# Another order for the unit schedule of a fused attention and feed-forward kernel: other engines for casts and transposes, v loads ahead of q and k, more zero matmuls

## The chip, the cores and the metric

The kernel runs on one core of a Trainium2 chip. Times are device microseconds (us) of one execution, input in HBM to output in HBM; the figure that is compared is the median of the runs. In the profile the engines are PE (TensorE's matmuls), PEld (its weight loads), DVE (VectorE), ACT (ScalarE), POOL (GpSimd) and SP (SyncE, which only issues transfers). Every engine works through its own queue in order, and waits on semaphores for the others.

## The reference

Attention with 4 batches, 8 heads, 768 positions and a head size of 64, followed by a feed-forward layer on 3072 tokens of width 512:

```python
scores = scale * np.matmul(q, k.transpose(0, 1, 3, 2))
keep = is_global | is_local          # k among the first 8, or 0 <= q - k < 96
scores = np.where(keep, scores - slope[h] * dist, -1e9)
a = softmax(scores)
x = (a @ v)  -> [3072, 512]
h = np.maximum(np.maximum(x @ w1, x @ w2), x @ w3)     # 512 -> 768, three times
out = h @ w_out                                        # 768 -> 512
```

A query sees at most its own block of 128 positions, the one before, and the first 8 positions of its batch. All inputs and the output are float32; the kernel computes in bfloat16 with float32 sums.

## The kernel before

The tokens are cut into 24 tiles T of 128 (six to a batch, t = T mod 6). The program is a list of short units, `SCHEDULE`, and the loop of lines 475 and 476 emits them one after the other. Units of one engine run in the order of the list; nothing reorders them. Each unit writes tiles from pools with few buffers (lines 102 to 117), and an instruction that needs a buffer waits until its last reader is done. The last number of most units names an engine: 0 ScalarE, 1 VectorE, 2 GpSimd; 3 and 4 have meanings of their own.

Loads, all issued by SyncE in list order: `l n.s` (`load_part`, line 158) loads a part of q or k for a group of tiles; groups 0, 1 and 2 are the tile pairs 0-1, 2-3 and 4-5, with part 0 the q and part 1 the k; groups 3 and 4 are tiles 6-9 and 10-11. `L T` loads q and k of one later tile, `v T` its v, `w g.j` and `o i` the feed-forward weights. The parts l0.0 and l0.1 are issued ahead of the list (lines 439 and 440).

Casts to bfloat16: `c` (line 183) and `C T.0` (line 198; 3 splits it between VectorE and GpSimd) for q and k, `C T.1` (line 189) for v, `W` and `Q` for weights. Transposes of q and k into `qkT`: `x n.s` (lines 239 and 243) and `X T` (lines 261 to 266) on PE with a copy out of PSUM, where `x` with 3 uses one VectorE copy and with 4 one half copy each by ScalarE and VectorE; `X T.4` is instead one DMA transpose issued by SyncE (line 250), with no PE work and no copy.

Attention of tile T: `S T.g` is the scores of four heads, each score bank (psS, tags sp0 and sp1, one buffer each) holding two key blocks, and the exponential on ScalarE (line 288). With a 1 at its end the mask is added by two PE matmuls of a bias (line 275); with a 0 the product is masked by `M T.g` on VectorE (line 307). `K h` and `B h` make the mask and the bias of head h out of distances. `G` and `V` copy the first eight keys and values of the batch into the previous tile's place (lines 214, 216, 221). `A T.b` multiplies by v into score bank b (lines 322 and 325) and divides on VectorE (lines 331 and 332) into `xb`. `T T` transposes the result into `xT`: on PE with a copy (lines 349 and 350) or, with 4, by a DMA transpose (line 340).

Feed-forward, on chunks of 4, 2, 2, 4, 4, 4 and 4 tiles: `F c.f.j` is one of three products for one of six 128-wide parts of the hidden layer, four matmuls (line 361) into one of three `psH` buffers; j = 0 is copied out by ScalarE (line 366), j = 1 and 2 are folded in by VectorE maxima (lines 368 and 370). `O c.i` is a tile's output (six matmuls, line 376), its copy (line 382) and its store by SyncE (line 383). `E` is the last chunk's output. `D i.n` issues n matmuls of zeros (line 436).

Of the kernel before, what the change touches and what calls it, by code (L numbers as in the profile page):

```python
# [22 lines left out]


SCHEDULE = """
    K0 K1 K2 K3 K4 K5 l1.0 l1.1 D0.3 c0.0.2 B0.1 B1.1 B2.1 B3.0 K6 B4.1 B5.1 c0.1.1 c1.0.2 x0.0.4 B6.1
    B7.1 x0.1.4 S0.0.1 v0 l2.0 l2.1 K7 S0.1.1 G0.0 S1.0.1 S1.1.0 x1.0.3 c1.1.2 M0.0 M0.1 M1.0 v1 x1.1.4
    C0.1.2 v2 A0.1 G1.2 S2.0.1 M1.1 c2.0.2 x2.0.1 C1.1.1 S2.1.0 G2.2 S3.0.1 M2.0 M2.1 C2.1.1 T0.1 S3.1.1
    M3.0 M3.1 c2.1.2 v3 A1.0 C3.1.0 w0.0 V1.2 x2.1.2 w1.0 A2.1 V2.2 A3.0 T1.0 T2.1 T3.1 W1.0.1 W0.0.0
    G3.2 S4.0.0 S4.1.0 F0.0.0 F0.1.0 M4.0 F0.2.0 F0.3.0 G4.1 S5.0.0 M4.1 S5.1.0 w0.1 W0.1.1 w0.2 W0.2.2  # L30
    V3.2 F0.0.1 F0.1.1 F0.0.2 F0.1.2 v4 C4.1.0 A4.0 V4.2 w1.1 W1.1.2 W2.0.0 F0.4.0 F0.5.0 M5.0 M5.1 w1.2
    W1.2.2 v5 W2.1.0 T4.0 F0.2.1 F0.3.1 l3.0 l3.2 F0.4.1 l3.1 c3.0.2 c3.2.2 F0.5.1 o2 C5.1.0 A5.1 l3.3
    F0.2.2 Q2.2 F0.3.2 W2.2.0 o0 T5.0 F0.4.2 o1 F0.5.2 x3.0.0 F1.0.0 F1.1.0 c3.1.1 F1.2.0 x3.2.0 Q0.2
    F1.0.1 F1.1.1 F1.2.1 l4.0 l4.1 c3.3.0 F1.0.2 F1.1.2 F1.2.2 x3.1.2 x3.3.1 F1.3.0 F1.4.0 Q1.2 F1.3.1
    S6.0.0 S6.1.0 v6 v7 v8 G6.0 F1.3.2 F1.5.0 v9 c4.0.1 F1.4.1 S7.0.0 S7.1.0 G7.2 v10 M6.0 M6.1 M7.0
    M7.1 O0.0.0 F1.4.2 c4.1.1 C6.1.2 C7.1.2 L12 F1.5.1 S8.0.0 S8.1.0 x4.0.0 O0.1.0 A6.0 x4.1.2 A7.1 V7.2
    F1.5.2 v11 T6.0 O0.2.0 T7.1 G8.2 C8.1.2 S9.0.0 S9.1.0 G9.1 v12 v13 O0.3.0 F2.0.0 F2.1.0 S10.0.0 M8.0
    M8.1 M9.0 M9.1 S10.1.0 C9.1.2 L13 L14 F2.0.1 F2.1.1 F2.0.2 A8.0 C12.0.1 F2.1.2 G10.2 O1.0.0 V8.2
    A9.1 X12.1 M10.0 M10.1 C10.1.0 C11.1.0 F2.2.0 S11.0.0 S11.1.0 M11.0 M11.1 L15 F2.3.0 F2.4.0 O1.1.0
    V9.2 A10.1 F2.2.1 V10.2 T8.0 F2.3.1 F2.5.0 T9.0 A11.1 F2.4.1 T10.0 F2.2.2 F2.3.2 T11.1 F2.4.2  # L40
    S12.0.0 S12.1.0 F2.5.1 C13.0.2 C14.0.2 C15.0.1 X13.4 F3.0.0 F3.1.0 F3.0.1 G12.1 C12.1.0 F3.2.0
    F3.1.1 F3.2.1 S13.0.0 S13.1.0 F2.5.2 v14 C13.1.0 C14.1.2 M12.0 M12.1 F3.0.2 F3.1.2 X14.4 F3.2.2
    X15.4 G13.2 M13.0 M13.1 S14.0.0 S14.1.0 F3.3.0 F3.4.0 F3.5.0 M14.0 M14.1 G14.1 A12.0 A13.1 F3.3.1
    F3.4.1 F3.5.1 S15.0.0 M15.0 S15.1.0 G15.0 v15 V13.2 L16 L17 v16 T12.4 v17 M15.1 O2.0.0 C15.1.0 A14.0
    V14.2 F3.3.2 F3.4.2 T13.4 F3.5.2 C16.1.0 C16.0.2 X16.3 T14.4 C17.0.2 A15.1 X17.4 O2.1.0 S16.0.0
    S16.1.0 G16.1 L18 V15.2 L19 T15.1 M16.0 O3.0.0 M16.1 F4.0.0 F4.1.0 F4.0.1 F4.1.1 C18.0.2 L20 C19.0.2
    A16.1 F4.2.0 F4.3.0 S17.0.0 S17.1.0 F4.2.1 F4.0.2 F4.3.1 v18 M17.0 v19 M17.1 X18.3 X19.4 C20.0.0
    V16.2 F4.1.2 C17.1.2 O3.1.1 A17.1 F4.2.2 F4.3.2 S18.0.0 M18.0 S18.1.0 M18.1 F4.4.0 T16.4 T17.4
    F4.4.1 C18.1.2 C19.1.1 F4.4.2 X20.4 G18.1 S19.0.0 S19.1.0 F4.5.0 L21 M19.0 M19.1 v20 F4.5.1 A18.0
    T18.4 F4.5.2 A19.1 T19.4 V19.1 C21.0.1 X21.4 G19.1 L22 C22.0.2 L23 X22.4 O3.2.1 O3.3.0 O4.0.1  # L50
    S20.0.0 S20.1.0 M20.0 G20.0 O4.1.0 F5.0.0 F5.1.0 F5.2.0 S21.0.0 S21.1.0 G21.2 F5.0.1 F5.1.1 M20.1
    M21.0 F5.3.0 F5.0.2 F5.1.2 F5.2.1 F5.2.2 v21 C20.1.1 C21.1.2 F5.4.0 S22.0.0 M21.1 S22.1.0 C23.0.0
    F5.3.1 M22.0 M22.1 F5.5.0 F5.3.2 A20.0 V20.2 G22.2 v22 F5.4.1 X23.4 v23 F5.5.1 T20.4 A21.1 V21.1
    T21.4 F5.4.2 F5.5.2 S23.0.0 S23.1.0 M23.0 O4.2.0 M23.1 C22.1.2 A22.0 C23.1.0 O4.3.0 V22.2 T22.4
    A23.1 T23.4 O5.0.1 O5.1.0 O5.2.1 O5.3.0 F6.0.0 F6.1.0 F6.0.1 F6.0.2 F6.2.0 F6.3.0 F6.4.0 F6.1.1
    F6.2.1 F6.1.2 F6.3.1 F6.4.1 F6.2.2 F6.3.2 F6.5.0 F6.4.2 F6.5.1 F6.5.2 E
"""


# [1 line left out]
def kernel(  # L61
# [272 lines left out]

    def u_XT(T, how):
        c, i = where[T]
        if i == 0:
            xT[c] = xT_pool.tile([128, NP, len(chunks[c]) * 128], BF16, name="xT", tag="xT")
        if how == 4:
            nc.sync.dma_start_transpose(out=xT[c][:, :, i * 128:(i + 1) * 128],  # L340
                                        in_=xb[T].rearrange("p h d -> p (h d)"))
            return
        if early(T):
            tp = psH.tile([128, NP, 128], BF16, name="xtp", tag="h")
        else:
            tp = psT.tile([128, NP, 128], BF16, name="xtp", tag="tp")
        x = xb[T].rearrange("p h d -> p (h d)")
        for jp in range(NP):
            nc.tensor.transpose(tp[:, jp], x[:, jp * 128:(jp + 1) * 128], identb)  # L349
# [4 lines left out]

    def u_F1(c, f, j):
        W = len(chunks[c]) * 128
        if f == 0 and j == 0:
            ht[c] = ht_pool.tile([128, NF, W], BF16, name="ht", tag="ht")
        ps = psH.tile([128, W], FP32, name="h", tag="h")
        for dm in range(4):  # L360
            nc.tensor.matmul(ps, w123[f // 2][:, dm, j, (f % 2) * 128:(f % 2) * 128 + 128],  # L361
                             xT[c][:, dm], start=(dm == 0), stop=(dm == 3))
# [147 lines left out]
```

## Time and profile before

| What | Value |
|---|---|
| median of 3 runs | 180.04 us (179.69 to 180.06) |
| span of the profiled execution | 178.3 us, first to last instruction |
| the profiled execution's own total | not given by the page; the runs' median is 1.74 us over the span |
| PE busy | 166.9 us, 94% |
| VectorE, ScalarE, GpSimd busy | 118.9, 103.1, 37.5 us |
| mean granted TensorE clock | 0.997 |
| moved by DMA | 35.52 MB, mean 199 GB/s |
| DMA transposes issued by SyncE | 11 into xT, 9 into qkT |

Busy time is the union of an engine's instructions, and matmuls overlap one another, so a mean duration of a matmul is longer than what it takes of PE. The start of a row is counted from the span's beginning. An "idle before" names what ended an engine's wait. The chain of waits is followed back from the last instruction, each step to what released it.

### The profile page before, as it was taken

The numbers are of one execution on the slowest core, as the hardware profiler recorded it, in microseconds if no ns is written. First come the engines' busy times: TensorE is split into PE (matmuls) and PEld (weight loads), VectorE is DVE, ScalarE is ACT, GpSimd is POOL, SyncE is SP. The second block draws the span as 40 slices with busy tenths as digits, with TensorE's granted clock in tenths as the row PEclk, the third lists the DMA queues.
The fourth block names the chain that finished last, engine by engine and source line by source line (L and its number), as shares of the span: only waits on it lengthen the run. The fifth ranks groups of instructions, "written<-read, shape, count | busy, mean of one in ns | idle before, by whom it ended". The sixth has DMA issues, their size and how long they took to land.

```text
span 178.3 us, 3960 instructions
## 1 busy us (share of the span) xinstructions
PE 166.9 (94%) x1529; PEld 95.8 (54%) x1551; DVE 118.9 (67%) x237; ACT 103.1 (58%) x160; POOL 37.5 (21%) x65
## 2 busy tenths in 40 slices
PE   3599799999999999999999999999999999999992
PEld 0455644558867677845555555545444555444442
DVE  4519875986787689748979447979358896136620
ACT  4867898646689858555744837351772643341122
POOL 4355203543343112310007024100020401000000
PEclk9999999999999999999999999999999999999998
DMA  5999999999998999989544999769889674610006
GB/s 140 292 271 242 357 320 384 320 361 358 251 193 213 229 254 236 174 171 233 94 90 118 159 247 235 157 132 186 173 153 294 136 143 146 224 42 4 0 11 226
DMA packets 83587, 35.52 MB, mean 199 GB/s; under 512 B 66160, under 2 KB 78320, under 8 KB 83568
## 3 DMA queue, kind: packets, MB, share of 16 engines
q1 hardware_dynamic: 83424, 35.20, 82.8%
q8 instruction: 12, 0.20, 0.5%
q10 hardware_dynamic: 144, 0.07, 0.1%
q14 instruction: 7, 0.06, 0.1%
HBM read 25.17 MB, written 6.29 MB: 176 GB/s over the span
## 4 chain that ended last, share of the span: by engine, by line
PE 85%; DMA 8%; SPq 2%; issue 1%; POOL 1%; DVE 1%; ACT 1%; ACTq 0%
PE h L361 53%; PE po L376 17%; PE sp L283 6%; DMA rawv<-in_v_dram 4%; DMA rawp<-in_q_dram 4%; PE op L322 3%; PE op L325 2%; SPq L174 2%; PE tpp L239 2%; PE xtp L349 1%; SPq L158 1%; POOL qkp L183 1%; PE tp L261 1%; DVE xb L332 0%; ACT va L189 0%
## 5 line engine op out<-in xcount | busy, mean ns | idle before, releaser
L361 PE MATMUL h<-xT,w 128*128 128x512 bf16 (+1 forms) x491 | 99.2, 348 | 0.7 <-issue 0.2
L361 PEld LDWEIGHTS <-w 128*128 128x128 bf16 x504 | 46.9, 98 | 40.5 <-DVE w L427 0.3
L288 ACT ACTIVATE P<-sp 128x1024 bf16<-128x1024 f32 (+1 forms) x48 | 43.4, 955 | 20.6 <-PE sp L283 20.4
L368 DVE TENSOR_TENSOR h<-h,h 128x512 bf16<-128x512 bf16 (+1 forms) x42 | 25.3, 610 | 25.7 <-PE h L361 16.5
L366 ACT CAST h<-h 128x512 bf16<-128x512 f32 (+1 forms) x42 | 21.6, 533 | 21.5 <-PE h L361 21.3
L376 PE MATMUL po<-wo,ht 128*128 128x512 bf16 (+2 forms) x147 | 33.1, 362 | 0.5
L370 DVE TENSOR_TENSOR ht<-h,h 128x512 bf16<-128x512 bf16 (+1 forms) x42 | 25.1, 607 | 3.7 <-PE h L361 3.0
L307 DVE TENSOR_TENSOR P<-P,wmask 128x1024 bf16<-128x1024 bf16 x36 | 24.8, 718 | 3.6 <-ACT P L288 3.5
L376 PEld LDWEIGHTS <-ht 128*128 128x128 bf16 x156 | 14.0, 98 | 13.9
L382 ACT COPY ost<-po 128x512 f32<-128x512 f32 (+2 forms) x20 | 11.2, 564 | 17.8 <-PE po L376 17.7
L332 DVE TENSOR_TENSOR xb<-op,rz 128x512 bf16<-128x512 f32 x24 | 16.6, 692 | 0.8
L283 PEld LDWEIGHTS <-qkT 64*128 64x128 bf16 x352 | 10.2, 96 | 10.0 <-issue 8.0
L283 PE MATMUL sp<-qkT 64*128 64x128 bf16 x352 | 15.2, 223 | 0.4 <-DVE xb L332 0.4
L322 PEld LDWEIGHTS <-P 128*128 128x128 bf16 x192 | 12.5, 97 | 2.5 <-ACT P L288 0.2
L221 POOL COPY va<-vaf 8x260 int32<-8x260 int32 x14 | 6.3, 452 | 34.5 <-PE op L325 34.5
L198 POOL CAST qkb<-raw 128x1024 bf16<-128x1024 f32 x7 | 7.2, 1037 | 27.7 <-DMA raw<-in_q_dram 18.9
L322 PE MATMUL op<-va,P 128*128 128x65 bf16 x160 | 12.3, 193 | 0.7 <-ACT va L189 0.6
L239 PE MATMUL tpp<-identb,qkp 128*128 128x128 bf16 x96 | 8.5, 246 | 4.0 <-POOL qkp L183 3.4
L325 PEld LDWEIGHTS <-P 128*128 128x128 bf16 x160 | 10.4, 97 | 2.2 <-issue 0.7
L239 PEld LDWEIGHTS <-qkp 128*128 128x128 bf16 x96 | 7.0, 111 | 5.8 <-POOL qkp L183 4.3
L325 PE MATMUL op<-va,P 128*128 128x65 bf16 x128 | 9.9, 193 | 0.0
L243 ACT COPY qkT<-tpp 128x1024 bf16<-128x1024 bf16 (+1 forms) x9 | 7.9, 874 | 3.4 <-PE tpp L239 3.4
(66 smaller groups left out, 107.5 us busy)
## 6 DMA issues: line engine op xcount, KB each, us to landing
rawv<-in_v_dram SPq DMA_DIRECT2D x24, 256.0 KB, 4.8
out_dram<-ost SPq DMA_DIRECT2D x23, 256.0 KB, 2.3
rawp<-in_q_dram SPq DMA_DIRECT2D x6, 512.0 KB, 7.2
rawp<-in_k_dram SPq DMA_DIRECT2D x6, 512.0 KB, 7.4
wst<-in_moe_w_dram SPq DMA_DIRECT2D x3, 1024.0 KB, 9.7
raw<-in_q_dram SPq DMA_DIRECT2D x12, 256.0 KB, 4.1
raw<-in_k_dram SPq DMA_DIRECT2D x12, 256.0 KB, 4.8
wst<-in_moe_w_dram SPq DMA_DIRECT2D x3, 512.0 KB, 8.7
```

Of the source, the lines that this page charges most:

```text
L239: nc.tensor.transpose(tp[:, e, j - lo], qb["p", n, s][:, e, 2 * j:2 * j + 2].rearrange("i h d -> i (h d)"), identb)
L283: nc.tensor.matmul(sp[:, hh, j2, ds], qT(T - ds, 1)[hsl, jp], qT(T, 0)[hsl, jp], start=not how, stop=True, skip_group_check=True)
L288: nc.scalar.activation(P[:, :, 0:n], sp.rearrange("p a b d n -> p (a b) d n")[:, :, 0:n], AF.Exp, bias=0.0, scale=scale)
L307: nc.vector.tensor_mul(P, P, wmask[:, g, :, 0:2])
L322: nc.tensor.matmul(o, P[:, i, 0], heads(va[T])[:, h], start=True, stop=(t == 0), skip_group_check=True)
L325: nc.tensor.matmul(o, P[:, i, 1], heads(va[T - 1])[:, h], start=False, stop=True, skip_group_check=True)
L332: nc.vector.tensor_tensor(out=x.rearrange("p (g h) d -> p g h d", g=2), in0=o4[:, :, :, 0:64], in1=rz[:, :, :, None].to_broadcast([128, 2, ...
L361: nc.tensor.matmul(ps, w123[f // 2][:, dm, j, (f % 2) * 128:(f % 2) * 128 + 128], xT[c][:, dm], start=(dm == 0), stop=(dm == 3))
L366: nc.scalar.copy(h01, ps)
L368: nc.vector.tensor_max(h01s[c, f], h01s[c, f], ps)
L370: nc.vector.tensor_max(ht[c][:, f], h01s[c, f], ps)
L376: nc.tensor.matmul(po, ht[c][:, f, tt * 128:(tt + 1) * 128], wo[:, f, cols], start=(f == 0), stop=(f == NF - 1))
```

## The change

The list is another one: 487 units in place of 483. What differs, beside a general shuffle of neighbouring units:

- SyncE's queue begins l1.0 l1.1 v0 v1 v2 l2.0 l2.1 v3 where it was l1.0 l1.1 v0 l2.0 l2.1 v1 v2 v3; v4 stands behind w1.1; the parts of group 3 come in the order 3, 0, 1, 2.
- The first two casts (c0.0, c0.1) are both VectorE's, c1.1 too; v of tile 3 is cast by VectorE and stands in the list ahead of A2. Five of the eight bias products are GpSimd's, two ScalarE's. The scores of tile 1 come before those of tile 0, S1.1 with the bias matmuls, S3.0 without.
- There are 13 zero matmuls in five places in place of 3 in one: D1.2, D0.4 and D4.4 ahead of the first transposition, D2.2 between S2.1 and S3.0, D3.1 ahead of the first F. `D` with n = 0 issues nothing (not used).
- T8, T9, T10 and X18 are DMA transposes where they were PE's. X16 keeps PE's transposes, with one copy by ScalarE where it had two halves.
- Other casts, small copies, outputs and the banks of some A change engine or place; seven `V` go from GpSimd to ScalarE. F parts of a chunk are no longer taken in ascending order, so `xT` and `ht` are allocated at the first unit of a chunk, whichever it is.

Line numbers of the functions move by 1 to 3. The diff, with the list cut to what is spoken of:

```diff
 SCHEDULE = """
-    K0 K1 K2 K3 K4 K5 l1.0 l1.1 D0.3 c0.0.2 B0.1 B1.1 B2.1 B3.0 K6 B4.1 B5.1 c0.1.1 c1.0.2 x0.0.4 B6.1
-    B7.1 x0.1.4 S0.0.1 v0 l2.0 l2.1 K7 S0.1.1 G0.0 S1.0.1 S1.1.0 x1.0.3 c1.1.2 M0.0 M0.1 M1.0 v1 x1.1.4
-    C0.1.2 v2 A0.1 G1.2 S2.0.1 M1.1 c2.0.2 x2.0.1 C1.1.1 S2.1.0 G2.2 S3.0.1 M2.0 M2.1 C2.1.1 T0.1 S3.1.1
-    M3.0 M3.1 c2.1.2 v3 A1.0 C3.1.0 w0.0 V1.2 x2.1.2 w1.0 A2.1 V2.2 A3.0 T1.0 T2.1 T3.1 W1.0.1 W0.0.0
-    G3.2 S4.0.0 S4.1.0 F0.0.0 F0.1.0 M4.0 F0.2.0 F0.3.0 G4.1 S5.0.0 M4.1 S5.1.0 w0.1 W0.1.1 w0.2 W0.2.2
...
-    V9.2 A10.1 F2.2.1 V10.2 T8.0 F2.3.1 F2.5.0 T9.0 A11.1 F2.4.1 T10.0 F2.2.2 F2.3.2 T11.1 F2.4.2
...
-    F4.4.1 C18.1.2 C19.1.1 F4.4.2 X20.4 G18.1 S19.0.0 S19.1.0 F4.5.0 L21 M19.0 M19.1 v20 F4.5.1 A18.0
...
+    D1.2 K6 B5.1 D0.4 c0.0.1 B1.2 B6.2 K1 K7 l1.0 K3 c0.1.1 K5 K0 D4.4 B4.0 B2.2 B0.2 K4 K2 B3.0
+    B7.2 x0.0.3 l1.1 x0.1.4 S1.0.1 c1.0.2 S1.1.1 G0.2 v0 v1 x1.0.4 S0.0.1 M0.0 S0.1.1 M0.1 c1.1.1
+    x1.1.4 G1.2 v2 C0.1.2 A0.1 l2.0 S2.0.1 l2.1 S2.1.0 G2.2 M2.0 D2.2 S3.0.0 C2.1.1 M2.1 M3.0 T0.1
+    C1.1.2 S3.1.1 M3.1 v3 M1.0 M1.1 A1.0 C3.1.1 V1.0 c2.0.2 x2.0.0 c2.1.2 A2.1 V2.0 x2.1.2 A3.0 T1.0
+    T2.0 w0.0 G3.2 S4.1.0 W0.0.1 T3.1 S4.0.0 w1.0 D3.1 F0.1.0 F0.0.0 G4.2 S5.0.0 S5.1.0 M4.1 W1.0.1
+    W2.0.1 w0.1 W0.1.1 w0.2 w1.1 M5.0 F0.3.0 F0.5.0 F0.1.1 F0.0.1 W0.2.2 V3.2 M4.0 F0.1.2 F0.0.2 v4
+    C4.1.0 F0.2.0 W2.1.0 W1.1.2 F0.4.0 v5 w1.2 W1.2.2 l3.3 M5.1 A4.0 c3.3.2 F0.2.1 l3.0 c3.0.2 V4.0
...
+    F1.4.0 C6.1.2 A7.1 V7.0 M8.0 M6.1 O0.2.1 M8.1 G8.0 S9.1.0 S9.0.0 O0.1.1 L14 M9.0 F1.5.2 F1.4.1
...
+    C11.1.2 M10.0 F2.1.0 O0.0.1 C12.0.2 F2.3.0 A9.1 V9.1 O1.1.0 T9.4 T8.4 M10.1 C10.1.0 G10.2
+    S11.1.0 S11.0.0 X12.1 F2.1.1 F2.3.1 C13.0.1 F2.5.0 C14.0.0 X13.4 M11.1 A10.1 M11.0 T10.4 F2.4.0
+    O1.0.0 V10.0 F2.3.2 X14.4 v15 G12.0 v13 v12 S12.0.0 S12.1.0 L18 F2.1.2 L16 C15.0.1 F2.4.1 F2.5.1
+    F2.0.0 A11.1 X15.4 F2.2.0 F2.2.1 v14 F2.0.1 F2.4.2 T11.1 v17 S13.1.0 S13.0.0 F2.5.2 F3.5.0
...
+    X18.4 F3.4.2 C14.1.2 A14.1 C17.1.0 X16.0 v18 T14.4 F3.1.1 F3.1.2 C17.0.1 F3.5.2 C19.0.0 X19.4
+    S16.0.0 S16.1.0 v19 O3.2.0 V14.0 X17.4 O2.0.0 O3.0.0 G18.0 M15.1 M16.1 C16.1.1 v20 A15.1 O3.1.1
+    S18.1.0 S18.0.0 M18.0 T15.1 L20 O3.3.0 L21 S19.0.0 S19.1.0 F4.1.0 M18.1 F4.4.0 G16.1 M16.0 V15.1
...
 """
@@ u_XT
-        if i == 0:
+        if c not in xT:
@@ u_F1
-        if f == 0 and j == 0:
+        if c not in ht:
@@ u_D
-    def u_D(i, n):
+    def u_D(i, n=0):
+        if n == 0:
+            return
```

More of the change, by code (lines that the diff above doesn't have):

```diff
@@ L31 @@
[L31 to L39, printed above, removed]
-    V9.2 A10.1 F2.2.1 V10.2 T8.0 F2.3.1 F2.5.0 T9.0 A11.1 F2.4.1 T10.0 F2.2.2 F2.3.2 T11.1 F2.4.2
@@ L41 @@
[L41 to L45, printed above, removed]
@@ L46 @@
-    S16.1.0 G16.1 L18 V15.2 L19 T15.1 M16.0 O3.0.0 M16.1 F4.0.0 F4.1.0 F4.0.1 F4.1.1 C18.0.2 L20 C19.0.2
-    A16.1 F4.2.0 F4.3.0 S17.0.0 S17.1.0 F4.2.1 F4.0.2 F4.3.1 v18 M17.0 v19 M17.1 X18.3 X19.4 C20.0.0
-    V16.2 F4.1.2 C17.1.2 O3.1.1 A17.1 F4.2.2 F4.3.2 S18.0.0 M18.0 S18.1.0 M18.1 F4.4.0 T16.4 T17.4
-    F4.4.1 C18.1.2 C19.1.1 F4.4.2 X20.4 G18.1 S19.0.0 S19.1.0 F4.5.0 L21 M19.0 M19.1 v20 F4.5.1 A18.0
-    T18.4 F4.5.2 A19.1 T19.4 V19.1 C21.0.1 X21.4 G19.1 L22 C22.0.2 L23 X22.4 O3.2.1 O3.3.0 O4.0.1
@@ L51 @@
[L51 to L55, printed above, removed]
@@ L56 @@
-    F6.2.1 F6.1.2 F6.3.1 F6.4.1 F6.2.2 F6.3.2 F6.5.0 F6.4.2 F6.5.1 F6.5.2 E
+    D1.2 K6 B5.1 D0.4 c0.0.1 B1.2 B6.2 K1 K7 l1.0 K3 c0.1.1 K5 K0 D4.4 B4.0 B2.2 B0.2 K4 K2 B3.0
[3 more added lines that the diff above has]
+    T2.0 w0.0 G3.2 S4.1.0 W0.0.1 T3.1 S4.0.0 w1.0 D3.1 F0.1.0 F0.0.0 G4.2 S5.0.0 S5.1.0 M4.1 W1.0.1
@@ new lines @@
+    W2.0.1 w0.1 W0.1.1 w0.2 w1.1 M5.0 F0.3.0 F0.5.0 F0.1.1 F0.0.1 W0.2.2 V3.2 M4.0 F0.1.2 F0.0.2 v4
+    C4.1.0 F0.2.0 W2.1.0 W1.1.2 F0.4.0 v5 w1.2 W1.2.2 l3.3 M5.1 A4.0 c3.3.2 F0.2.1 l3.0 c3.0.2 V4.0
+    C5.1.0 W2.2.0 F0.3.1 F0.4.1 l3.1 c3.1.2 A5.0 T4.0 F0.5.1 F0.2.2 T5.0 l3.2 F0.3.2 o0 o2 v7 o1
+    x3.3.0 F1.1.0 F1.2.0 F1.1.1 x3.0.0 F1.1.2 F1.0.0 x3.1.2 F0.4.2 l4.1 v6 c3.2.2 x3.2.0 v8 F1.3.0
+    F1.3.1 F1.3.2 S6.1.0 S6.0.0 F1.5.0 C7.1.1 Q0.1 F1.0.1 v9 v11 l4.0 S7.1.0 S7.0.0 L13 c4.1.0 G6.1
@@ new lines @@
+    F1.2.1 M7.1 F1.5.1 M7.0 L12 F0.5.2 v10 G7.2 S8.1.0 S8.0.0 F1.2.2 F1.0.2 M6.0 x4.1.4 Q1.2 Q2.2
+    F1.4.0 C6.1.2 A7.1 V7.0 M8.0 M6.1 O0.2.1 M8.1 G8.0 S9.1.0 S9.0.0 O0.1.1 L14 M9.0 F1.5.2 F1.4.1
+    A6.1 C8.1.2 A8.0 G9.2 T7.0 c4.0.2 x4.0.2 O0.3.1 T6.0 M9.1 C9.1.1 F1.4.2 S10.0.0 S10.1.0 V8.1 L15
+    C11.1.2 M10.0 F2.1.0 O0.0.1 C12.0.2 F2.3.0 A9.1 V9.1 O1.1.0 T9.4 T8.4 M10.1 C10.1.0 G10.2
+    S11.1.0 S11.0.0 X12.1 F2.1.1 F2.3.1 C13.0.1 F2.5.0 C14.0.0 X13.4 M11.1 A10.1 M11.0 T10.4 F2.4.0
+    O1.0.0 V10.0 F2.3.2 X14.4 v15 G12.0 v13 v12 S12.0.0 S12.1.0 L18 F2.1.2 L16 C15.0.1 F2.4.1 F2.5.1
@@ new lines @@
+    F2.0.0 A11.1 X15.4 F2.2.0 F2.2.1 v14 F2.0.1 F2.4.2 T11.1 v17 S13.1.0 S13.0.0 F2.5.2 F3.5.0
+    F3.3.0 F3.3.1 M12.0 F3.3.2 F3.4.0 F2.0.2 L17 v16 F3.5.1 F2.2.2 G13.2 S14.0.0 S14.1.0 C12.1.1
+    M12.1 M13.1 F3.0.0 M14.0 M14.1 M13.0 F3.4.1 G14.0 F3.2.0 L19 F3.0.1 C13.1.2 C15.1.2 A13.0 A12.1
+    C16.0.3 F3.2.1 O2.1.0 V13.0 F3.2.2 S15.0.0 S15.1.0 C18.0.0 T13.4 F3.1.0 F3.0.2 G15.0 M15.0 T12.4
+    X18.4 F3.4.2 C14.1.2 A14.1 C17.1.0 X16.0 v18 T14.4 F3.1.1 F3.1.2 C17.0.1 F3.5.2 C19.0.0 X19.4
+    S16.0.0 S16.1.0 v19 O3.2.0 V14.0 X17.4 O2.0.0 O3.0.0 G18.0 M15.1 M16.1 C16.1.1 v20 A15.1 O3.1.1
@@ new lines @@
+    S18.1.0 S18.0.0 M18.0 T15.1 L20 O3.3.0 L21 S19.0.0 S19.1.0 F4.1.0 M18.1 F4.4.0 G16.1 M16.0 V15.1
+    M19.0 A16.0 T16.4 M19.1 G19.2 F4.2.0 F4.1.1 F4.2.1 C18.1.0 S17.1.0 M17.1 S17.0.0 V16.2 C20.0.2
+    F4.2.2 C19.1.0 L22 M17.0 F4.0.0 F4.0.1 X20.4 A19.1 A18.0 T19.4 F4.5.0 F4.5.1 F4.1.2 T18.4 F4.3.0
+    A17.1 C20.1.0 T17.4 C21.0.1 F4.4.1 F4.3.1 F4.3.2 F4.5.2 F4.4.2 S20.0.0 S20.1.0 C22.0.3 F4.0.2
+    F5.3.0 G20.0 M20.0 M20.1 F5.1.0 F5.1.1 X21.4 S21.0.0 S21.1.0 L23 X22.4 F5.3.1 v23 F5.0.0 C23.0.1
@@ L57 @@
+    v22 V19.2 A20.0 M21.1 F5.0.1 F5.0.2 F5.1.2 X23.4 v21 C21.1.2 G21.0 S22.1.0 S22.0.0 G22.1 M21.0
+    F5.2.0 C23.1.0 M22.1 F5.4.0 V20.1 F5.4.1 S23.0.0 M23.0 S23.1.0 F5.4.2 M22.0 O4.2.0 F5.2.1 O4.3.1
+    A21.1 T21.4 T20.4 O4.1.0 C22.1.0 F5.3.2 V21.2 F5.2.2 A22.0 T22.4 F5.5.0 O4.0.0 V22.2 M23.1 A23.0
+    T23.4 F5.5.1 F5.5.2 O5.1.0 O5.3.0 O5.0.0 F6.4.0 F6.4.1 F6.0.0 F6.4.2 F6.0.1 F6.0.2 F6.5.0 F6.3.0
+    F6.1.0 F6.1.1 F6.3.1 F6.2.0 F6.1.2 F6.2.1 O5.2.1 F6.2.2 F6.3.2 F6.5.1 F6.5.2 E
 """
```

## The prediction

> **What bounds the kernel now.** I read the page's busy line and slices first, then five stretches of the span, then the chain of waits up to the first feed-forward matmul, then the queue of SyncE and the starts of the waiting engines.
>
> ```profile
> span 178.3 us, 3960 instructions
> ...
> PE 166.9 (94%) x1529; PEld 95.8 (54%) x1551; DVE 118.9 (67%) x237; ACT 103.1 (58%) x160; POOL 37.5 (21%) x65
> ...
> PE   3599799999999999999999999999999999999992
> ```
>
> ```profile
> 0.00:23.44 23.44, 16.59 (x208) 10.44 (x208) 14.66 (x41) 17.12 (x28) 9.38 (x23) 1.00 1.07 265
> 23.44:50.00 26.56, 26.40 (x231) 16.51 (x234) 19.48 (x34) 18.72 (x30) 9.02 (x10) 1.00 1.09 325
> 50.00:100.00 50.00, 49.53 (x556) 31.73 (x566) 38.61 (x82) 34.52 (x55) 11.63 (x20) 1.00 0.88 179
> 100.00:150.00 50.00, 49.53 (x419) 25.22 (x424) 36.14 (x67) 25.75 (x37) 7.45 (x12) 1.00 0.87 182
> ```
>
> The columns of the second view are length, then busy time of PE, PEld, DVE, ACT and POOL, granted clock, DMA share and GB/s. PE lacks 6.85 us in the first 23.44 us, but only 0.16 + 0.47 + 0.47 = 1.10 us in the next 126.56. So from 23.44 us on only less PE work shortens the run, and before that only an earlier first feed-forward matmul does. The chain says what that matmul waits for:
>
> ```profile
> 13.07 7.08 DMA rawv<-in_v_dram
> 20.16 0.02 issue
> 20.18 0.63 ACT va L189
> ...
> 21.54 0.22 DVE rz L331
> 21.75 0.02 issue
> 21.78 0.70 DVE xb L332
> 22.48 0.05 issue
> 22.52 0.40 PE xtp L349 x4
> 22.92 0.55 PE sp L283 x16
> 23.48 0.34 PE h L361
> ```
>
> It is v of tile 3, the tenth load of SyncE's queue, which lands at 20.16. Its cast, its attention product (A3), the division and the transposition (T3) follow, and F0 starts at 23.44.
>
> ```profile
> 8.56 1.04 POOL L183 CAST qkp<-rawp 128x1024 bf16<-128x1024 f32 x1 [2.53 <-DMA rawp<-in_q_dram]
> 10.40 1.04 POOL L183 CAST qkp<-rawp 128x1024 bf16<-128x1024 f32 x1 [0.80 <-DMA rawp<-in_k_dram]
> ...
> 13.38 1.04 POOL L183 CAST qkp<-rawp 128x1024 bf16<-128x1024 f32 x1 [0.96 <-DMA rawp<-in_q_dram]
> ```
>
> ```profile
> 10.09 4.85 SPq L174 DMA_DIRECT2D rawv<-in_v_dram  x3
> 14.98 4.33 SPq L417 DMA_DIRECT2D wst<-in_moe_w_dram  x4
> ```
>
> The loads land one after another (l1.0 8.54, l1.1 10.38, l2.0 13.36), each about 5.2 us after SyncE has finished issuing it; SyncE issues without a pause, at 1.2 to 1.9 us per load. The DMA engines are full.
>
> **The change part by part.** *Loads.* Before, SyncE issues l1.0 l1.1 v0 l2.0 l2.1 v1 v2 v3 and then the weights; after it, l1.0 l1.1 v0 v1 v2 l2.0 l2.1 v3 and the same weights. The same ten loads stand up to v3, so I take its landing as 20.16 again. Bounds: one v load took 1.17 us to issue and the others up to 1.87, so v3 may move by 0.7 either way. v1 and v2 come some 3.3 us earlier (l2.0 and l2.1 took 1.74 and 1.58), which nothing waits for at the end of the chain. l2.0 and l2.1 move back by v1 and v2, some 2.9 to 3.3 us: l2.0 from 13.36 to about 16.4, l2.1 from about 15.2 (issue end 10.04 + 5.2) to about 18.3. GpSimd casts l2.1 in 1.04 (19.4), PE transposes it in 0.45 (19.9), ScalarE copies it in 1.01 (20.9). A3 is queued on PE behind that transposition, and S4 needs the copy; both are ready before A3 can start.
>
> *From v3 to F0.* The cast goes from ScalarE (0.63) to VectorE (0.42): 20.58. But on VectorE it stands ahead of tile 2's division, which thus waits for v3 as well: reciprocal and product 0.92, to 21.5. A3's own pair follows, to 22.4. T3's four transposes end near 22.9. VectorE has the cast of w0.0 (0.69) ahead of T3's copy: 22.4 to 23.1, then 0.42, so F0 starts at 23.5. Against 23.44 that is +0.05. Ends: -0.3 (the w0.0 cast finds a gap) and +0.7 (v3 0.7 later). v4 goes behind w1.1: w0.2 was cast at 27.48, and 2.25 MB land from there to 34.1, 337 GB/s, so v4 lands near 31.2, and after ScalarE's 0.63 its A4 could start at 31.9. PE arrives there after ten F0 groups of 0.86 and S5's 0.55, at 32.7. Hidden by 0.8.
>
> *Zero matmuls: 13 for 3.* Ten stand at the start. The three of before took 1.46, one each 0.42 with 0.63 for the last, so ten run from 1.19 to about 5.6. The first cast, now on VectorE (4.95 + 0.69 = 5.64), covers them. Two more (0.43 at full rate) stand among the scores of tiles 2 and 3, one (0.22) where PE waits for T3's copy: all ahead of F0, in 6.85 us that PE idles. Cost 0; without that cover up to 3.4 us of PE work.
>
> *The first scores.* Five bias products move from VectorE (0.35 each) to GpSimd, where the trace has none. Lower end VectorE's 0.35, upper end GpSimd's cast of 1024 columns, 1.04; a cast of 512 took 0.61, so I take 0.6. They end between 5.5 and 9 us, 0.6 giving 6.7, and the bias matmuls of S1 come near 8.3. Two bias products and eight masks on ScalarE (0.43 to 0.51) end near 8.1. S1 goes ahead of S0. Following ScalarE's queue from 8.8 (eight exponentials, 6 x 1.03 and 2 x 0.59, two half copies 0.59, V1 and two copies of 1.0), it ends near 20.8, 0.7 before tile 2's division. S1.1 takes its mask from PE (two matmuls, 0.43) and S3.0 from VectorE (0.69): an exchange with no sum.
>
> *Early matmuls at half rate.* Two bias matmuls took 1.03 us at 10.27 but 0.59 at 14.14. What PE does from 6.08 to 13.9 costs it 7.8 us, perhaps 3.9 too much. It stands ahead of v3's landing, so a faster PE gains nothing there, and I take 0. The Trainium skill (TensorE: Matmul & The Clock Gate, Part 1: The HAM clock gate) says that some 3.4 us of sustained activity release the half clock, and the ten zero matmuls look made for that; if PE's rate set the start, the sum would be 3.9 us lower. The rows agree with the rule, and the chain denies the gain.
>
> *Transposes moved to DMA.* T8, T9, T10 and X18 leave PE. The price of each:
>
> ```profile
> 72.96 0.22 PE xtp L349 x4
> ...
> 96.06 0.22 PE tp L261 x4
> 96.28 0.22 PE tpk L261 x4
> ```
>
> 3 x 0.22 + 0.44 = 1.10 us less PE work in stretches where PE idles 1%. This is the gain. ScalarE loses three copies of 0.59 and X18's 0.59, VectorE 0.42. On SyncE's queue four transposes of about 1.25 us to issue are added; they land in 2.4 (xT) and 3.2 (qkT). Their readers come late: F3 starts 10.4, 10.4 and 7.6 us of PE work behind T8, T9 and T10, and S18 8.9 us behind X18. A load queued behind them (v15, v13, v12) is read over 10 us later. X16 keeps its eight transposes, with one copy of 1.02 on ScalarE for 0.59 and 0.42 on two engines.
>
> *Casts and small copies.* Seven 8-row copies of v go from GpSimd (0.45) to ScalarE (between 0.22, its 128x32 copy, and 0.37, its 128x256 one), about 2 us more in a queue 58% busy; others change engine for similar prices. GpSimd's queue has no run of casts that PE waits for. The allocation conditions issue nothing. Cost 0 while PE's own work covers it.
>
> *Order from 23.44 on.* PE's other work is the same, instruction for instruction. Each product A holds its score bank until VectorE has divided: 0.22 + 0.70 and gaps, 0.97 us by the chain. S9.1, S11.1 and S18.1 now follow A7, A9 and A15 with only one output group between (1.29 us by the chain's six matmuls): 0.32 us is left each time for VectorE being late. Before, the closest such place had 1.17 us (A9 to S11.1) and PE lost nothing. Ends 0 and 0.7 at each, when one VectorE piece of 0.69 to 0.7 stands ahead; I take 0.15 in all, nearer to what the old place showed.
>
> **The sum.** The profiled execution has 178.3 us of span; the page gives no total for it, and the runs' median of 180.04 (179.69 to 180.06) leaves 1.7 around it, which I keep. 178.3 + 0.05 - 1.10 + 0.15 = 177.4 of span, 179.1 us.
>
> **The rivals.**
> *A, slower: VectorE's queue makes PE wait for score banks.* VectorE has 38.6 us of work in 50.00:100.00. The new order puts more feed-forward maxima, mask products and outputs (O0 goes to it, 0.69 each) between 35 and 85 us. Once it runs 0.7 us late at the three places named, and likewise where A11, A16 and A20 wait behind fresh mask products, six stalls of up to 0.4 to 0.7 cost 2.4 to 4: 180.4 to 182.0, say 181.0. It decides once the stalls pass 1.4 us. For it: margins of 0.3. Against: before ran at 0.2 to 0.4 without loss. 24%.
> *B, the gain is lost at the start.* v3 lands 0.7 later, or w0.0's cast on VectorE waits for its load and T3's copy behind it too; F0 slips by 0.8 to 1.4. 180.0, between 179.7 and 180.4. 16%.
> *C, the start is shorter.* PE's rate, or ScalarE's queue, rather than v3 sets F0; with ScalarE done at 20.8 F0 could come 1 us earlier at most, the full 3.9 only if PE alone mattered. 178.0. For it: ten zero matmuls and v1, v2 earlier. Against: the chain. 10%.
> *The forecast,* 179.1, its own range 178.6 to 179.6: 50%.
>
> **How the numbers follow.** A measurement of this kernel tells 0.2%, 0.36 us, from no change. Faster: the forecast and C, 0.60. Same: most of B, 0.14. Slower: A and the rest of B, 0.26. The range from 178.0 to 181.2 takes in C's middle, B and most of A; some 10% lie on each side.
>
> **What would show it.** Right: v3's landing near 20.2 and F0's first matmul near 23.5; PE's idle time from there near 1.2 us; 14 transposes into xT and 10 into qkT on SyncE's queue; PE busy from F0 on lower by 1.1. Wrong: waits of PE's score matmuls on VectorE's xb, or on ScalarE, of some tenths each beyond 35 us (A); a later landing of v3 or a w0.0 cast that waits (B); F0 before 23 us (C).

## The result, and the profile after

The changed kernel takes 182.64 us (median of 4 runs, 182.45 to 182.98) against 180.05 us (179.69 to 180.21) before: a ratio of 1.0148, with an interval of 1.0133 to 1.0164. It is 2.6 us slower. The forecast was 179.1 us, faster by 0.9. The profiled execution took 182.98 us, with this busy line and row of slices:

```profile
span 181.2 us, 3931 instructions
...
PE 169.5 (94%) x1517; PEld 95.2 (53%) x1541; DVE 121.5 (67%) x234; ACT 104.9 (58%) x167; POOL 37.3 (21%) x58
...
PE   7498899999979999999999999999989999999992
```

The span is 2.9 us longer. The view by stretches (length, then busy time of PE, PEld, DVE, ACT and POOL, granted clock, DMA share, GB/s) is cut where the first feed-forward matmul F0 starts, at 25.41 us, and where PE loses most:

```profile
0.00:25.41 25.41, 19.92 (x217) 10.80 (x218) 14.86 (x36) 18.54 (x30) 14.64 (x27) 0.87 1.07 271
25.41:50.00 24.59, 24.38 (x223) 15.17 (x227) 17.44 (x30) 17.89 (x29) 8.11 (x9) 1.00 1.05 309
50.00:55.00 5.00, 4.08 (x54) 3.00 (x53) 4.95 (x9) 4.57 (x7) 4.21 (x5) 1.00 0.95 226
55.00:100.00 45.00, 44.48 (x473) 28.09 (x478) 37.13 (x77) 28.44 (x47) 5.82 (x10) 1.00 1.03 207
100.00:135.00 35.00, 34.50 (x302) 17.41 (x306) 24.51 (x47) 19.65 (x32) 3.17 (x5) 1.00 1.12 198
135.00:140.00 5.00, 4.43 (x46) 2.22 (x42) 4.28 (x9) 4.41 (x7) 0.61 (x1) 1.00 0.60 120
```

Two things are to be seen. F0 starts 1.97 us later than before (23.44). And PE, which lacked 1.10 us between 23.44 and 150 us before, now lacks 0.21 + 0.92 + 0.52 + 0.50 + 0.57 and 0.05 in 140 to 150, 2.77 us. The 1.10 of before, and about as much of the 2.77, are matmuls missing from the trace: PE's view of waits before shows none over 0.2 us from F0 on, and the changed kernel's trace has 1517 of PE's records where two of the runs below, which issue the same matmuls, have 1541. PE's view of waits after the change names the two real stalls from F0 on, those of 50 to 55 (0.87 us) and 135 to 140 us (0.52 us):

```profile
PE tpp L240 <- DVE ht L371: 0.9, 1, 0.9
PE h L362 <- DVE h L369: 0.5, 1, 0.5
```

The last group of output matmuls gives the sum. It ends 5.37 us after 172.52, at 177.89; before, 5.37 after 169.65, at 175.02. From F0 to there it is 152.48 us against 151.58, that is +0.90: the two stalls are 1.39, and about 0.5 of the rest is saved. With F0's 1.97 this is the 2.9 us of span. Against the forecast's 177.4 us of span it is 3.8 more: 1.9 in the start of F0, and 1.85 from there to the last matmul, 1.39 of them the two stalls. The other 0.46 is saving that the forecast counted on and this profile does not show; why is not traced.

The chain of waits up to F0 says what made F0 late (start, length, what; it counts a matmul from the end of the one before it, so F0 stands at 25.52 here and at 25.41 by its own start):

```profile
3.81 1.25 POOL bias L296
...
5.13 1.53 POOL bias L296
...
6.72 1.41 POOL bias L296
...
8.19 1.18 POOL bias L296
9.41 1.01 PE sp L276 x2
...
16.81 1.95 ACT P L289 x2
18.78 2.44 DVE P L308 x2
21.22 0.34 DVE xT L351
...
22.39 0.34 DVE va L190
...
23.72 0.70 DVE xb L333
24.47 0.40 PE xtp L350 x4
24.87 0.33 PE sp L284 x8
25.20 0.32 PE wp L439
25.52 0.27 PE h L362
```

The load of v of tile 3, which carried the chain before, is not in it any more. In its place stand four bias products on GpSimd, one after the other, and after the scores two mask products on VectorE of 1.2 us each. GpSimd's own rows around them:

```profile
3.81 6.79 POOL L296 TENSOR_SCALAR bias<-rbase 128x384 bf16<-128x384 f32 x5 [0.75 <-DVE rbase L473]
10.66 1.04 POOL L184 CAST qkp<-rawp 128x1024 bf16<-128x1024 f32 x1
...
18.20 2.48 POOL L184 CAST qkp<-rawp 128x1024 bf16<-128x1024 f32 x2
```

The transfers issued show that the change does what it says: 14 transposes into xT and 10 into qkT (count, and the median from issue to landing).

```profile
xT<-xb SPq DMA_TRANSPOSE x14, 2.5
qkT<-qkb SPq DMA_TRANSPOSE x10, 4.2
```

### The profile page after: what moved, and what is told of

The parts are those of the page before. It is cut to its first block, busy times and chain, and to the rows that moved or that the text cites. A ratio compares the mean times of both kernels' runs of the same rounds, so it can differ in the third digit from the quotient of the medians.

```text
span 181.2 us, 3931 instructions
## 1 busy us (share of the span) xinstructions
PE 169.5 (94%) x1517; PEld 95.2 (53%) x1541; DVE 121.5 (67%) x234; ACT 104.9 (58%) x167; POOL 37.3 (21%) x58
## 4 chain that ended last, share of the span: by engine, by line
PE 80%; DVE 7%; POOL 4%; DMA 3%; issue 2%; ACT 2%; SPq 1%; POOLq 0%; DVEq 0%
PE h L362 46%; PE po L377 17%; PE sp L284 6%; DMA raw<-in_k_dram 3%; POOL bias L296 3%; DVE P L308 3%; PE op L323 3%; PE op L326 2%; PE tpp L240 2%; PE sp L276 2%; ACT P L289 1%; DVE xb L333 1%; PE xtp L350 1%; DVE h L369 1%; DVE ht L371 1%
## 5 line engine op out<-in xcount | busy, mean ns | idle before, releaser
L308 DVE TENSOR_TENSOR P<-P,wmask 128x1024 bf16<-128x1024 bf16 x36 | 27.2, 769 | 4.2 <-ACT P L289 4.2
L383 ACT COPY ost<-po 128x512 f32<-128x512 f32 (+2 forms) x18 | 9.9, 556 | 24.2 <-PE po L377 19.8
L217 POOL COPY qkT<-kg 128x32 bf16<-128x32 bf16 x9 | 2.9, 318 | 51.9 <-PE sp L284 27.0
L244 ACT COPY qkT<-tpp 128x1024 bf16<-128x1024 bf16 (+1 forms) x11 | 9.4, 857 | 1.7 <-PE tpp L240 1.7
L184 POOL CAST qkp<-rawp 128x1024 bf16<-128x1024 f32 x8 | 8.7, 1097 | 2.0 <-DMA rawp<-in_k_dram 1.0
L240 PEld LDWEIGHTS <-qkp 128*128 128x128 bf16 x96 | 6.5, 105 | 4.7 <-DVE qkp L184 2.9
```

Source lines behind the costliest of these rows:

```text
L240: nc.tensor.transpose(tp[:, e, j - lo], qb["p", n, s][:, e, 2 * j:2 * j + 2].rearrange("i h d -> i (h d)"), identb)
L308: nc.vector.tensor_mul(P, P, wmask[:, g, :, 0:2])
```

## The experiments

The theory after the result had three parts: GpSimd's bias products make F0 late (called G in the expectations), GpSimd's w_out casts stretch VectorE's mask products beside them (W), and the transposes save what the forecast said. All edits below are to the changed kernel's list, unless the kernel before is named. The medians of the kernel before, run beside them, lay between 180.01 and 180.11.

**The bias products back on VectorE.**

```diff
-    B5.1 D0.4 c0.0.1 B1.2 B6.2 K1
+    B5.1 B1.1 B2.1 B0.1 D0.4 c0.0.1 B6.1 B7.1 K1
...
-    B4.0 B2.2 B0.2 K4 K2 B3.0 B7.2 x0.0.3
+    B4.0 K4 K2 B3.0 x0.0.3
```

> The changed kernel with its five bias products of GpSimd given back to VectorE (B1, B2, B0 ahead of the first cast, B6 and B7 behind it). Theory G: the five products, 1.3 us each on GpSimd, hold S1 until 9.4 and GpSimd's casts until 10.7, and the two microseconds by which F0 came late are theirs: F0 starts near 23.5, time 180.6 to 181.0. Theory Q: VectorE's own queue between S2's exponential and F0 (6.6 us without a pause in the changed kernel) sets F0, whatever the first scores do: F0 at 24.7 or later, time 182.0 or more. Theory L (the loads of l2 come too late): no change, 182.6.

Measured: 181.83 us (180.57 to 183.26, 6 runs), a ratio of 1.012 (1.0083 to 1.0157); the profiled execution is the 180.57. Its chain of waits:

```profile
9.18 0.54 PE sp L275 x2
...
12.55 7.21 DMA rawv<-in_v_dram
...
19.79 0.43 DVE va L189
...
21.96 0.40 PE xtp L349 x4
...
23.01 1.14 PE h L361 x5
```

F0 starts 2.5 us earlier than in the changed kernel, at 22.89 (23.01 as the chain counts it), and the chain again starts from the landing of v of tile 3 (19.76). Moving the bias products removes the late start. Part of the 2.5 us may be the clock's: two bias matmuls take 0.54 us here and took 1.01 at 9.41 us in the changed kernel, whose granted clock was 0.50 from 7.65 to 14.47 us. The run with both mends and three zero matmuls, below, parts the two. The median fell by only 0.8, because the times spread: the executions with a granted clock of 0.991 took 182.2 to 183.3, those at 1.00 took 180.6 to 181.4.

**The old order of the loads** (l2.0 and l2.1 ahead of v1 again).

```diff
-    v0 v1 x1.0.4 ... A0.1 l2.0 S2.0.1 l2.1 S2.1.0
+    v0 l2.0 l2.1 v1 x1.0.4 ... A0.1 S2.0.1 S2.1.0
```

> The changed kernel with SyncE's loads in the old order, v0 l2.0 l2.1 v1 v2 v3. Theory L: l2 earlier brings x2 and A3 earlier, F0 by 0.5 or more, time 182.1 or less. Theories G and Q: GpSimd reaches the casts of l2 only at 18.2, behind a copy that waits for S2.1, so l2 lands in time either way: 182.4 to 182.9, F0 at 25.4.

Measured: 182.80 us (182.67 to 182.96), F0 at 25.26. The order of the loads has no visible part in it.

**Three zero matmuls at the start, and no others.**

```diff
-    D1.2 K6 ... D0.4 ... D4.4 ... D2.2 ... D3.1
+    K6 ... D0.3
```

> The changed kernel with three zero matmuls at the start, as before the change, and none later. Theory Z: the ten at the start bring the clock up and the gap behind them lets it fall, and the first scores pay for that; without them F0 moves by 0.5 us or more, either way. Theories G and Q: the first scores wait for the bias, not for PE; only the last zero matmul, 0.3 us right ahead of F0, counts: 182.2 to 182.7.

Measured: 182.96 us (182.47 to 183.49), F0 at 25.55. The chain is again that of GpSimd's bias products and of two mask products (2.64 us), and two bias matmuls take 1.01 us, as in the changed kernel. In this kernel the ten extra zero matmuls neither help nor cost more than the spread.

**The four DMA transposes alone, in the kernel before.**

```diff
-    T8.0 ... T9.0 ... T10.0 ... X18.3
+    T8.4 ... T9.4 ... T10.4 ... X18.4
```

> The kernel before with T8, T9, T10 and X18 as DMA transposes and nothing else changed. The forecast's term: 1.10 us less PE work where PE does not idle, 178.7 to 179.1. Rival: SyncE's queue or the landing gives it back (loads behind the transposes come late, F3 waits for T10): 179.7 to 180.5.

Measured: 183.29 us (181.85 to 184.28), a ratio of 1.0173 (1.0135 to 1.0212), slower than before by 3.2. PE's view of waits:

```profile
PE xtp L349 <- DVE xb L332: 3.4, 1, 3.4
```

And VectorE's row for that xb, and two stretches with the clock behind the wait:

```profile
76.05 0.69 DVE L332 TENSOR_TENSOR xb<-op,rz 128x512 bf16<-128x512 f32 x1 [3.71 <-DMA xT<-xb]
```

```profile
75.00:80.00 5.00, 3.21 (x22) 1.91 (x23) 2.69 (x7) 1.08 (x2) 0.00 (x0) 0.71 0.67 133
80.00:85.00 5.00, 5.00 (x24) 2.12 (x22) 1.98 (x5) 2.27 (x4) 0.62 (x1) 0.95 0.94 194
```

Tile 11's transposition is still PE's; its xb comes late, since VectorE waited 3.71 us for a DMA transpose to be done with a buffer of xb, whose pool has three. The clock then fell as well; the three executions at 1.00 took 181.9 to 182.7 us, the three at 0.991 took 183.9 to 184.3. In the old order the transposes have no room. Their price can still be estimated: from F0 (23.47) to the last matmul (179.13) it is 155.66 us; less the wait of 3.39 and the 1.7 that the two stretches lack of the full clock, 150.6 are left, 1.0 less than the 151.58 of before.

**The w_out casts out of the mask products' way.** In the changed kernel the two casts stand on GpSimd behind G7.2, a small copy that waits 7.87 us for PE.

```diff
-    F0.5.2 v10 G7.2 ... x4.1.4 Q1.2 Q2.2 F1.4.0
+    F0.5.2 v10 Q1.2 Q2.2 G7.2 ... x4.1.4 F1.4.0
```

> The changed kernel with one edit: GpSimd's two casts of w_out (the units Q1.2 and Q2.2) stand ahead of tile 7's copy on GpSimd's queue (G7.2), which waits 7.87 us for TensorE in the changed kernel, instead of behind it; their loads landed long before, so they run in that idle stretch near 42 us and not at 50.27. Theory W: the mask products M7.1 and M8.0 on VectorE, 1.46 and 1.19 us in the changed kernel beside the two casts, were stretched by them, and the 0.92 us that TensorE idles in 50 to 55 us come from that. It expects these products at 0.7 to 0.8 us, TensorE idle less than 0.3 in that stretch, and 181.8 (0.9 below 182.6). Rival O: VectorE's queue alone is too long there (five other operations between 49 and 55 us), and the casts add little: products still over 1.1, the idle time stays, 182.4 to 182.8. Rival P: the products get short, but TensorE then waits for the same thing a step later: 182.3 to 182.8 with the idle time moved.

Measured: 181.72 us (181.66 to 182.61), a ratio of 1.011 (1.0092 to 1.0128), 0.9 below the changed kernel. VectorE and GpSimd in the changed kernel, in order of time:

```profile
50.39 1.46 DVE L308 TENSOR_TENSOR P<-P,wmask 128x1024 bf16<-128x1024 bf16 x1
...
52.10 1.19 DVE L308 TENSOR_TENSOR P<-P,wmask 128x1024 bf16<-128x1024 bf16 x1
```

```profile
50.11 0.21 POOL L217 COPY qkT<-kg 128x32 bf16<-128x32 bf16 x1 [7.87 <-PE h L362]
50.27 2.48 POOL L431 CAST wo<-wost 128x1024 bf16<-128x1024 f32 x2
```

And with the edit:

```profile
50.52 0.69 DVE L307 TENSOR_TENSOR P<-P,wmask 128x1024 bf16<-128x1024 bf16 x1
...
51.45 0.77 DVE L307 TENSOR_TENSOR P<-P,wmask 128x1024 bf16<-128x1024 bf16 x1
```

```profile
46.91 2.02 POOL L430 CAST wo<-wost 128x1024 bf16<-128x1024 f32 x2 [4.79 <-DMA wost<-in_moe_w_out_dram]
```

The mask products return to 0.69 and 0.77 and PE has no idle time between 50 and 55 us. So the stretched products were the cause there. (The expectation was wrong in one thing: the casts ran at 46.9 and not at 42, since their loads had only just landed.) The stall of 135 to 140 us went too, and one of 0.46 us appeared ahead of it, for the landing of tile 17's DMA transpose.

**The same, with C23.0 on GpSimd.**

```diff
-    C23.0.1 v22 V19.2
+    C23.0.2 v22 V19.2
```

> The same, and the cast of the group C23.0 on GpSimd instead of on VectorE, where it waited 1.50 us for k's load at 133.10 with tile 20's division, M21.1 and a feed-forward maximum behind it. Theory K: this wait is what TensorE's 0.57 us of idle time in 135 to 140 us comes from: that goes, and the time is 0.4 to 0.6 below the run with the w_out casts alone (181.3 if that gives 181.8). Rival: the wait passes to whoever reads the cast (the transposes of tile 23 and then its scores), or VectorE is late there without it: within 0.2 of the run with the w_out casts alone.

Measured: 184.36 us (183.38 to 187.21), slower by 2.6 than without it. GpSimd's rows near the end:

```profile
122.58 0.61 POOL L196 CAST qkb<-raw 128x512 bf16<-128x512 f32 x1 [5.92 <-DMA raw<-in_k_dram]
133.01 1.04 POOL L198 CAST qkb<-raw 128x1024 bf16<-128x1024 f32 x1 [9.81 <-DMA raw<-in_k_dram]
133.99 0.39 POOL L221 COPY va<-vaf 8x260 int32<-8x260 int32 x1
```

The cast waits for its load on GpSimd's queue, and the small copy V19.2 behind it, which ran at 123.28 in the changed kernel, now runs at 133.99. PE waited 2.87 us for it. The edit moved a wait into a queue where something else was due. That C23.0's wait on VectorE caused the 0.52 us at 135 to 140 us therefore remains argued, not shown.

**The four transposes back on PE.**

```diff
-    A9.1 V9.1 O1.1.0 T9.4 T8.4 ... F2.1.1 ... T10.4 F2.4.0 O1.0.0 ... X18.4
+    A9.1 V9.1 T8.0 O1.1.0 ... F2.1.1 T9.0 ... F2.4.0 O1.0.0 T10.0 ... X18.3
```

> The changed kernel with the transposes of tiles 8, 9 and 10 and of the q/k group 18 back on TensorE (T8.0, T9.0, T10.0, X18.3), placed so that their inputs are done when TensorE comes to them. It measures the one term of the forecast that made the change faster. If the forecast's 1.10 us is what the four transposes cost TensorE, 183.7. If TensorE's time in them lies in gaps that it had anyway, or if the four transfers on the DMA queue delay others, 182.4 to 182.9; below 182.4 the DMA transposes cost time.

Measured: 185.38 us (184.77 to 185.54), 2.74 above the changed kernel. PE's waits in it:

```profile
PE tp L261 <- ACT qkb L198: 0.9, 1, 0.9
PE tpp L239 <- DVE ht L370: 0.9, 1, 0.9
...
PE xtp L349 <- DVE qkT L266: 0.3, 1, 0.3
```

The middle one is the stall of 50 to 55 us that the changed kernel has too. The other two, 1.2 us, come from where the edit puts T9 and X18, and the changed kernel's stall of 135 to 140 us (0.52) is not there. From F0 (25.52) to the last matmul (180.22) it is 154.70 us against 152.48, 2.2 more, of which the waits make 0.7. That leaves about 1.5 us for the transposes and whatever else shifted: not less than the 1.10 of the forecast, but no clean price.

**Both mends and C23.0 on GpSimd.**

> The changed kernel with three parts undone or mended: the five bias products on VectorE, the two w_out casts ahead of G7.2, C23.0 on GpSimd. If the three causes are independent and make up what the prediction missed, the best runs lie near 180.57 - 0.9 = 179.7, perhaps 179.2 with C23.0, against 180.09 before: the gain of the transposes is then seen for the first time. If a shorter stretch only moves TensorE's wait along, 180.4 or more in the best runs. The run with the bias products on VectorE alone spread from 180.57 to 183.26, its higher times with a granted clock of 0.991 instead of 1.00; if this spread comes from the start, it is here too.

Measured: 183.89 us (181.65 to 184.73). PE waits 1.3 us for the same V19.2. The run repeats the fault of C23.0 and says nothing of the sum.

**Both mends** (the bias products on VectorE, the w_out casts ahead of G7.2).

> The changed kernel with the two mends that each worked alone: the five bias products on VectorE (the first feed-forward matmul then at 23.01 us instead of 25.4) and the two w_out casts ahead of tile 7's copy on GpSimd's queue (0.9 us less). C23.0 stays on VectorE. Theory: the two are independent, so 182.6 - 2.4 - 0.9 = 179.3 in the runs whose early matmuls run at the full clock, below the 180.0 of the kernel before. Rival: the run that also had C23.0 on GpSimd came to 181.65 at best, and if that is due to these two together and not to C23.0, this one gives 181.5 or more.

Measured: 181.30 us (180.95 to 183.21). It misses the 179.3: with F0 at 23.29, PE needs G7.2's copy 2 us sooner, but the w_out load on GpSimd's queue ahead of it lands no sooner. The copy ran at 50.74, and PE stood from 49.5 to 51.5. Stretches of one microsecond of this execution, which took 183.21:

```profile
50.00:51.00 1.00, 0.00 (x0) 0.00 (x0) 1.00 (x2) 0.92 (x1) 1.00 (x2) 1.00 0.55 122
51.00:52.00 1.00, 0.54 (x12) 0.54 (x12) 0.93 (x2) 0.22 (x2) 0.96 (x2) 0.68 0.84 184
52.00:53.00 1.00, 1.00 (x10) 0.60 (x7) 0.00 (x0) 1.00 (x2) 0.62 (x1) 0.50 1.02 225
53.00:54.00 1.00, 1.00 (x7) 0.71 (x5) 0.42 (x1) 0.84 (x1) 0.00 (x0) 0.50 0.95 185
54.00:55.00 1.00, 1.00 (x12) 0.98 (x11) 0.79 (x3) 0.38 (x1) 0.00 (x0) 0.61 1.14 329
```

After the pause of 1.92 us the granted clock is 0.50 for some 3 us, which costs another 1.7 us of full clock in the last four rows. The mends are not independent.

**Both mends with three zero matmuls.**

> The same with three zero matmuls at the start and no others, as before the change. Theory D: the spread of the run with the bias products on VectorE (180.57 to 183.26) comes from the clock gate, which the ten zero matmuls open near 5.6 us and which in some executions falls again in TensorE's pause near 7 us. Without them all executions run the early matmuls at half rate: a spread under 0.7 us, and a median of 179.3 to 179.9, since v of tile 3 sets the start in either case. Rival: the spread comes from elsewhere and stays over 1.5 us. If the early rate does set the start here, 180.3 or more.

Measured: 181.83 us (181.35 to 182.37), F0 at 24.38 instead of 23.29. Without the zero matmuls the start is 1.1 us later here, and its chain runs again through the first scores and two mask products of 2.66 us, and not through v of tile 3: with the bias products out of the way PE's early rate does set F0, the case that the expectation priced at 180.3 or more. Against the run with three zero matmuls and GpSimd's bias products (25.55), F0 is 1.2 us earlier: that much of the start is the bias products' alone, and the rest comes only together with the zero matmuls. The spread is smaller (1.0 us), but as the low clock of the run above lies at 51 to 55 us, the start is not its only source.

**The same, with tile 17's transposition on PE.**

```diff
-    T17.4 C21.0.1 F4.4.1 F4.3.1 F4.3.2
+    C21.0.1 F4.4.1 F4.3.1 T17.1 F4.3.2
```

> The same as the run with three zero matmuls, and tile 17's transposition on TensorE two output groups of the feed-forward later, instead of on the DMA queue behind two others, where TensorE waited 0.46 us for its landing. It adds 0.22 us of TensorE work and takes the wait away: 0.2 to 0.3 less than the run with three zero matmuls, 179.0 to 179.7. If the wait passes to another transposition, the same or 0.2 more.

Measured: 181.49 us (181.29 to 181.82), 0.3 less, as expected for the difference. F0 is at 23.88 in this profile, so the zero matmuls were worth 0.6 to 1.1 us of start, and the bias products without them 1.2 to 1.7.

**Both mends, tile 17 on PE, all zero matmuls of the change and four more in PE's early pause.**

```diff
-    x0.0.3 l1.1 x0.1.4
+    x0.0.3 D5.4 l1.1 x0.1.4
```

> The two mends and tile 17's transposition as in the run above, with all zero matmuls of the change and four more between the transposes of x0.0 and x0.1, where TensorE paused 1.2 us near 7 us. Theory D: the pause is where the gate falls, so bridged, all executions run the early matmuls at the full clock: spread under 0.7 us, median 178.9 to 179.3, granted clock 1.00. Rival: the gate falls elsewhere, and the spread stays over 1.5 us; or the four matmuls delay x0.1, and the time is over 179.8 with a small spread.

Measured: 180.92 us (180.37 to 181.25), a ratio of 1.004 (1.0025 to 1.0055), with clocks of 0.997 to 1.00 throughout, and F0 at 23.32. The spread is 0.9. PE still waits 0.63 us for G7.2's copy and 0.45 for a cast, both on GpSimd.

**The w_out casts in three places on GpSimd**, o0 and o2 ahead of G7.2, o1 behind it.

```diff
-    C7.1.1 Q0.1 F1.0.1 ... v10 Q1.2 Q2.2 G7.2 ... x4.1.4 F1.4.0
+    C7.1.1 F1.0.1 ... v10 Q0.2 Q2.2 G7.2 ... x4.1.4 Q1.2 F1.4.0
```

> The run with four more zero matmuls (180.92), with the w_out casts in three places on GpSimd: the first two loads to land (o0, o2) are cast ahead of tile 7's copy G7.2, the last (o1), which landed at 47.4 us and held that copy and with it the scores of tile 8 for 0.63 us, behind it; VectorE's cast of o0 goes. Theory I: after the mends TensorE still waits for GpSimd's in-order queue and for nothing else near 50 us, so its wait there goes and with it the drain of its pipeline: 0.6 to 0.9 less, 180.0 to 180.3. If one w_out cast beside a mask product is enough to make TensorE wait again: 180.7 to 181.1.

Measured: 180.50 us (179.79 to 181.97, 12 runs), a ratio of 1.0032 (1.001 to 1.0053). The 0.63 us of wait are gone; no wait over 0.3 us is left in the profile. F0 starts at 23.40 and the last matmul ends at 175.24: 151.84 us against the 151.58 of before. The start is again that of before, and what the transposes save is given back from F0 on; the waits that PE's view still names there, 0.3, 0.2 and 0.2 us, are part of it, and the rest is not traced.

**The same, with l4.0 ahead of v9 and v11.**

```diff
-    v9 v11 l4.0 S7.1.0
+    l4.0 v9 v11 S7.1.0
```

> The same, and the load l4.0 is issued ahead of v9 and v11, so that its cast on GpSimd (2.29 us behind its data) no longer holds the transposes x4.0, where TensorE waited 0.45 us near 58 us. Expected by the term of 1.10 us as the forecast has it: with the start at 23.3 us and no wait over 0.3 us, 179.3 to 179.7, below the 180.0 of the kernel before. If the term is not to be had because each transfer pulled ahead makes another late: within 0.3 of the run with the w_out casts in three places.

Measured: 180.69 us (179.73 to 181.27, 12 runs), 1.0029 (1.0012 to 1.0047): no gain. The wait of 0.45 us that the edit aims at was seen in the run with four more zero matmuls; the run just above, without the edit, does not have it either. PE's longest wait is now one of 0.7 us for an output copy on ScalarE. The second of the two outcomes named holds by its number.

No version beat the kernel before. The last two come within 0.3% of it, with single executions on both sides of 180.1. What is open is their spread of 1.5 to 2.2 us at granted clocks of 0.997 to 1.00, where the kernel before has 1.1 in 23 runs, and 0.4 without one of them, and so whether their mean could be brought below 180.

## Why the prediction was wrong

*Loads, and the way from v3 to F0: right in size, but hidden.* With the bias products mended, v3 landed at 19.76 (forecast 20.16) and F0 followed 3.13 us later (forecast 3.34). In the changed kernel neither was on the chain.

*"The first scores": the step that failed most.* I took 0.6 us for a bias product on GpSimd, between 0.35 and 1.04. It took 1.31, beyond the upper end, which was a cast of 1024 columns; a product with a scalar on 384 columns is dearer than that. And I let the range end in "between 5.5 and 9 us" without following 9 through S1, ScalarE and VectorE to F0. Scores at 9.41 instead of 8.3 made the exponentials that the chain runs through end at 18.76, and there the two mask products met two GpSimd casts and took 2.44 us for 1.4. The forecast had followed ScalarE's queue, but VectorE's only from v3's cast on; from 18.78 VectorE worked almost without a pause up to the last division ahead of F0. F0 came at 25.41; undoing the five products took 2.5 us off, 0.6 to 1.1 of it only together with the zero matmuls.

*"GpSimd's queue has no run of casts that PE waits for": wrong, and the 0 for casts with it.* It priced a cast by its own engine's time alone. Two w_out casts beside two mask products cost 0.9 us, shown by moving them. The trace of before could have warned: its mask products averaged 718 ns, above their 0.69, so some were already stretched. The seven small copies on ScalarE took 0.40 each, just over my upper end of 0.37; nothing waited for them.

*Zero matmuls and early rate: 0 was right for this kernel,* by the run with three. It was not right for the mended one, where they bring 0.6 to 1.1 us: what stood behind the bias products was not only v3. No profile shows GpSimd's bias products together with early matmuls at the full rate.

*Transposes, -1.10: borne out as PE's work, by estimate.* With the w_out casts moved, F0 at 25.53 and the last matmul at 176.63 leave 151.10 us against 151.58 before; less the wait of 0.46 for T17's transpose it is 150.64, that is 0.94 less work. The four transposes in the old order gave 1.0. What the forecast left out is that the order has to have room for them: no version kept the gain. And the 1.10 us of idle time that the forecast read from 23.44 on were missing records, so before the change there was still less to gain there than it said.

*"Order from 23.44 on", 0.15: mis-sized and misplaced.* None of S9.1, S11.1 and S18.1 waited. PE stood 0.87 us at the stretched mask products and 0.52 us for VectorE near 135 us, where C23.0's late cast is the argued cause.

Rival A had the right side, and VectorE's queue as what PE waits for behind F0, but its size was too small (180.4 to 182.0) and its mechanism was not the one: no score bank was waited for, and the larger part lay ahead of F0. Rival B looked for the delay at the start, in v3 and w0.0; it lay there, but in the bias products. The rival that was missing is GpSimd as a slow engine ahead of the first scores, and as a disturbance of VectorE.
